# Chunked attention and routed experts on one core: another order in the passage between the two halves, and the last half slot in two banks

## The chip, the cores and the metric

The kernel runs on one core of one Trainium2 chip, in one launch. The metric is the device time of an execution in microseconds; three runs of the kernel before gave a median of 430.8 us (430.32 to 432.37). All five engines (TensorE or PE, VectorE or DVE, ScalarE or ACT, GpSimd or POOL, and SyncE or SP, which here issues DMAs) work in the order in which the code emits their instructions: each engine takes its own instructions strictly one after the other and waits on semaphores for the others.

## The reference

The first half is attention in chunks: 4 batches, 8 heads, 768 rows, head dimension 64. A chunk of 32 queries sees 8 memory keys and at most 56 keys of its neighbourhood. The second half sends each of the 3072 rows (512 wide) to one of 8 experts, the one with the largest logit, and multiplies its output by the softmax weight of that expert.

```
for c in range(nc):                       # 24 chunks of 32
    k_full = concat(mem_k, k_ctx); v_full = concat(mem_v, v_ctx)
    scores = scale * q_c @ k_full.T
    a = exp(scores - max); a = a / (sum(a) + 1e-9)
    out[:, :, chunk] = a @ v_full
...
logits = x @ w_gate + modality_bias[modality_id]
e_idx = argmax(logits); gate_w = softmax(logits)[e_idx]
for e in range(8):
    h = relu(x[e_idx == e] @ w1[e])       # 512 -> 1024
    out[e_idx == e] = gate_w * (h @ w2[e])  # 1024 -> 512
```

## The kernel before

**Attention.** Two heads make a unit, so there are 16 units (`NU`), each in two halves; the loop at line 970 runs over the 32 halves and two steps more. In step i PE computes the scores of half i (`scores`, L328), turns the scores of half i-1 (`trans_p`, L345), turns the finished output of half i-2 (`trans_x`, L382) and multiplies half i-1 with its values (`attend`, L357). DVE subtracts the maximum (`less_max`, L336 and L339) and divides by the sums (`normalize`, L365 to L370, which writes `xb`). ACT takes the exponential (`PT`) and copies banks. POOL copies overlapping values inside a unit's value tile (`share_v`, L271), places the memory keys (`mem_keys`, L302) and stores finished rows to DRAM (`store_x`, L375). Value loads (`load_v`), query and key loads (`load_qk`) and all weights are issued by SP. `warm` (L283) puts products on an idle tile into PE's queue.

**Routing.** After the fourth unit of a batch its route is worked out by a generator (`route`, L529), of which the attention loop takes a few steps at a time (`pump`, L393). A step "full" marks a place where PE has work to emit. For the third batch (`b == B - 2`) the steps are: logits (L534, L543), the ranks of the tokens by a product with a triangle of ones (L575 to L580), on DVE `pick`, `rank`, `eb`, `first` (L583 to L598), on POOL five small operations that turn `first` into the register of the most frequent expert (L600 to L604), then `hi`, `lo`, `ac`, six pairs of indicator rows `l`, `a` (L670, L673: the first `NPOOL` = 2 pairs on POOL, the rest on DVE), the product of these that gives the table of tokens (L683), and its subtraction on DVE (`table`, L687). `gates` (L610) works out the gate values.

**Slots.** The second half works in slots of 256 tokens of one expert. A slot gathers its rows by an indirect DMA on POOL's queue (`gather`, L768: `ix`, `gx`, then two transfers into `xg`), turns them on PE (`trans`, L817), and splits them into a high and a low part (`xt`: ACT L819, DVE L820). Each weight tile is split too (`conv`: ACT L755 writes `wh`, DVE L756 writes `wl`). `mm1_first(f)` (L844) makes 12 products of 256 columns for one of 8 pieces of the hidden layer, its results go through ACT and DVE (L845, L846); `mm2` (L856) makes 48 products of 512 columns; ACT multiplies by the gate (L860) and POOL scatters the rows (L861). Slot 0 takes the most frequent expert of the first three batches, so that it can start before attention has ended: its table is the third batch's. `second` (L696) picks the expert of slot 1, and the rest of the routing runs beside slot 0 (`further`, L1132). Slots 1 to 11 follow (`slot`, L1180); `last_mm2` (L1251) ends slot 11, which is the last work of this input.

**What sets the order around the change.** No scheduler decides: the calls in the loop body and behind it are the order. PSUM tiles named `tr` rotate over four banks (`bank`, L84), `sc` and `av` over two each. For slot 0 the loop calls `gather(0)` at the end of step n-3, and `trans(0)`, `trans(1)` in step n, where they stand in PE's queue behind `trans_x` of half 30. `mm1_first(0)` and `(1)` follow the last `attend`.

Of the kernel before, what the change touches and what calls it, by code (L numbers as in the profile page):

```python
# [45 lines left out]
def tile_chunk_attention_top1_moe(  # L46
# [330 lines left out]
    def trans_x(u, hf):  # L377
        xb = xbs[u]
        t = bank()
        warm(t, {(NU - 2, 0): 3, (NU - 2, 1): 2, (NU - 1, 0): 2}.get((u, hf), 0))  # L380
        for i in range(3):
            nc.tensor.transpose(t[:, i * P:(i + 1) * P], xb[:, 3 * hf + i, :], ident)  # L382
        if hf == 0:
            xTs[u] = xall[:, u % 5]
        nc.scalar.copy(xTs[u][:, 384 * hf:384 * hf + 384], t[:, 0:384])
        if hf == 1 and not NU - 3 <= u < NU - 1:
            store_x(u)
# [141 lines left out]
    def route(b):  # L529
# [58 lines left out]
        if b == B - 2:  # L588

            cb, eb, oha = [sm.tile([P, E], F32, name=name, bufs=1) for name in ("cb", "eb", "oha")]  # L590
            top, ia, ib = [sm.tile([P, 1], F32, name=name, bufs=1) for name in ("top", "ia", "ib")]

            chosen.extend((cb, eb, oha, top, ia, ib))
            nc.scalar.copy(cb, rk[:, NT, :])
            pool, first = nc.gpsimd, sm.tile([P, 1], F32, name="first", bufs=1)
            nc.vector.scalar_tensor_tensor(eb, rk[:, NT, :], float(E), rev[:, 0], op0=ALU.mult, op1=ALU.add)
            yield "v"
            nc.vector.reduce_max(first, eb, axis=AX.X)  # L598
            yield "v"
            pool.tensor_scalar(top, first, 1.0 / E, -0.53125, op0=ALU.mult, op1=ALU.add)  # L600
            pool.tensor_scalar(top, top, MAGIC, -MAGIC, op0=ALU.add, op1=ALU.add)
            pool.tensor_scalar(ia, top, -float(E), first, op0=ALU.mult, op1=ALU.add)
            pool.tensor_scalar(regs0[:, 0:1], ia[0:1], -1.0, float(E), op0=ALU.mult, op1=ALU.add)
            pool.tensor_scalar(regs0[:, 1:2], ia[0:1], -float(HI), float(E * HI), op0=ALU.mult, op1=ALU.add)  # L604
# [43 lines left out]
        for t in range(NT):  # L648
# [28 lines left out]
            hot.append((l1, a1))  # L677
        if b == B - 2:
            yield from gates()
        yield "full"  # L680
# [6 lines left out]
        nc.vector.tensor_sub(table[:, 0:192], table[:, 0:192], tb[:, 0:192])  # L687
        yield "v"
        if b < B - 1:
            ts = sm.tile([P, E], F32, name="ts")  # L690
            nc.vector.reduce_sum(ts, oh.rearrange("p t e -> p e t"), axis=AX.X)
            yield "v"
            nc.vector.tensor_add(tot, tot, ts)
            yield "v"
# [275 lines left out]
    for i in range(n + 2):  # L970
# [9 lines left out]
        if i == n - 3:  # L980
            pump(2, late=True)
        if live:
# [14 lines left out]
        if u + 1 < NU and hf == 0:  # L997
# [5 lines left out]
            if u == 1:  # L1003
                blank_v(2)
            pump(1)
            store_k(u + 1, 1, 0, nc.scalar.copy)
# [7 lines left out]
        elif u + 1 < NU:  # L1014
            if u == 0:
                store_k(1, 0, 0, nc.scalar.copy)
            share_v(u + 1)
            trans_q(u + 1)
            store_q(u + 1, 0)
            store_q(u + 1, 1)  # L1020
            pump(3)
        elif live:
            pump(3)
        first = 2 <= i <= n
        if first:
# [3 lines left out]
        if i == n - 5:  # L1029
            pump(12, ("full",), late=True)  # L1030
        if i == n - 2:
            scores(*units[i + 1])
        if i == n:
            trans(0)
            trans(1)
            conv(1)
        if 1 <= i <= n:
            attend(*units[i - 1])
        if i == n - 3:
            while routing:  # L1040
                pump(99, ("full",), late=True)
        if i > n:
# [6 lines left out]
        if i in (n - 5, n - 4):  # L1049
            pump(2, late=True)  # L1050
        if i == n:
            mm1_first(0)
        if i >= n:
# [14 lines left out]
        if i == n - 5:  # L1068
            regroup_q(NU - 1)
        if i < n:  # L1070
            pump(1, ("tiled",))
# [31 lines left out]
        elif (u, hf) == (NU - 1, 1):  # L1103
            conv(0)
            other = second()
# [34 lines left out]
    keep(0)  # L1140
    mm1_first(2)
    for _ in other:
        pass
    gather(1)
    further()
    conv(4)
    mm1_first(3)
# [13 lines left out]
    for f in range(8):  # L1161
# [5 lines left out]
        if f == 5:  # L1167
            load_w(1, 1)
        if f > 2:
            further(2)  # L1170
            conv(f - 3)
        if f in (5, 6):
            trans(f - 5)
    store(0)
# [76 lines left out]
    def last_mm2(s):  # L1251
        tag, i, puts = ("av", "sc")[s % 2], s % 2, []
        for t in range(2):
            po = ps.tile([P, 512], F32, name=tag, tag=tag, bufs=2)
            for f in range(8):
                a, bb = hh[:, f, t * P:(t + 1) * P], hl[:, f, t * P:(t + 1) * P]
                for n, (x, w) in enumerate(((a, wh), (a, wl), (bb, wh))):
                    nc.tensor.matmul(po, x, w[8 + f], start=(f == 0 and n == 0), stop=(f == 7 and n == 2))
            o = hp.tile([P, DM], F32, name=f"o{t}", bufs=2)
            gate = gate_now[i][:, t:t + 1]  # L1260
            nc.scalar.activation(o, po, AF.Copy, scale=gate)
            puts.append(nc.gpsimd.indirect_dma_start(
# [69 lines left out]
```

## Time and profile before

| | |
|---|---|
| median of three runs | 430.8 us (430.32 to 432.37) |
| the profiled execution's own time | 429.93 us |
| its span, first to last instruction | 428.1 us |
| PE busy | 412.1 us, 96% of the span |
| DVE, ACT, POOL busy | 335.0, 300.2, 234.2 us |
| mean granted clock of TensorE | 0.996 |

The profiled execution took 429.93 us: its span of 428.1 us and 1.83 us around it. A busy time is the sum of an engine's instructions; PE's instructions overlap, and the ends of its products are modelled. Attention ends and slot 0 begins between 111 and 138 us of the span, slot 1 begins at 162, the last product starts at 421.3.

### The profile page before, as it was taken

How to read it: one execution, taken by the hardware profiler on the slowest of the kernel's cores; microseconds unless marked ns; L12 is line 12 of the kernel's file. 1: busy time of each engine (PE TensorE's matmuls, PEld its weight loads, DVE VectorE, ACT ScalarE, POOL GpSimd, SP SyncE). 2: the span in 40 equal slices, each digit the busy share in tenths (PEclk: the TensorE clock that was granted, in tenths of full speed). 3: DMA queues.
4: the chain of work that ended last, by engine and by line, in shares of the span. 5: the costliest groups of instructions: out<-in, count | busy, mean ns of one | idle time of the engine just before them, and what ended most of it. 6: DMA issues, size and time to landing. Idle time of an engine off the chain costs nothing.

```text
span 428.1 us, 11395 instructions
## 1 busy us (share of the span) xinstructions
PE 412.1 (96%) x3867; PEld 342.2 (80%) x3870; DVE 335.0 (78%) x800; ACT 300.2 (70%) x597; POOL 234.2 (55%) x320
## 2 busy tenths in 40 slices
PE   7998999999999999999999999999999999999993
PEld 4776788877867888899898888888888778888882
DVE  6899588588787789858979887868985887978750
ACT  7787778687655557557566867868784778878750
POOL 8967678669584409666753466452706566520101
PEclk9999999999999999999999999999999999999998
DMA  9889999999659500335423667979938323320101
GB/s 218 184 217 246 229 273 201 258 255 212 133 132 312 176 2 2 100 99 76 92 82 52 270 192 167 332 207 334 277 143 253 98 72 84 86 64 2 50 3 55
DMA packets 82543, 66.81 MB, mean 156 GB/s; under 512 B 50659, under 2 KB 71339, under 8 KB 82476
## 3 DMA queue, kind: packets, MB, share of 16 engines
q1 hardware_dynamic: 75276, 46.36, 44.4%
q0 software_dynamic: 6784, 19.50, 14.5%
q8 instruction: 33, 0.54, 0.6%
q14 instruction: 34, 0.28, 0.2%
q10 hardware_dynamic: 416, 0.13, 0.1%
HBM read 84.64 MB, written 12.76 MB: 228 GB/s over the span
## 4 chain that ended last, share of the span: by engine, by line
PE 57%; issue 16%; DVE 10%; DMA 6%; ACT 5%; POOL 4%; POOLq 0%; SPq 0%; ACTq 0%; DVEq 0%
PE av L856 11%; PE tr L844 9%; PE sc L856 8%; PE tr L825 7%; PE av L357 4%; PE tr L828 4%; PE sc L328 3%; ACT kbd L320 3%; PE tr L382 2%; PE tr L345 2%; DMA xpm<-xw 2%; PE tr L292 2%; PE tr L310 1%; DMA out_dram<-o,ix_now 1%; POOL xg L765 1%
## 5 line engine op out<-in xcount | busy, mean ns | idle before, releaser
L756 DVE TENSOR_TENSOR w<-raw,w 128x512 fp32r<-128x512 f32 x96 | 67.4, 746 | 4.1 <-ACT w L755 3.6
L825 PE MATMUL tr<-xt,w 128*128 128x512 f32 x256 | 70.3, 396 | 0.0
L856 PE MATMUL av<-wh,h 128*128 128x512 f32 x192 | 62.5, 398 | 0.0
L271 POOL COPY vw<-vw 24x1472 f32<-24x1472 f32 x32 | 45.0, 1408 | 18.9 <-DMA vw<-in_v_dram 17.5
L755 ACT CAST w<-raw 128x512 fp32r<-128x512 f32 x96 | 53.9, 619 | 0.6 <-DMA raw<-in_moe_w_dram 0.6
L856 PE MATMUL sc<-wh,h 128*128 128x512 f32 x160 | 51.7, 398 | 0.0
L825 PEld LDWEIGHTS tr<-xt,w 128*128 128x128 f32 x256 | 44.3, 189 | 7.5 <-DVE hs L834 0.7
L844 PE MATMUL tr<-xt,w 128*128 128x256 f32 x384 | 48.2, 285 | 1.2 <-DVE xt L820 0.7
L844 PEld LDWEIGHTS tr<-xt,w 128*128 128x128 f32 x384 | 46.8, 191 | 2.7 <-DVE xt L820 0.9
L320 ACT COPY kbd<-tr 64x672 f32<-64x672 f32 x57 | 44.6, 782 | 2.9 <-PE tr L314 1.3
L828 PEld LDWEIGHTS tr<-xt,w 128*128 128x128 f32 x256 | 39.3, 189 | 5.4
L856 PEld LDWEIGHTS av<-wh,h 128*128 128x128 f32 x192 | 36.1, 188 | 8.4 <-issue 0.2
L861 POOL DMA_INDIRECT out_dram<-o,ix_now x22 | 24.5, 1112 | 29.8 <-ACT o L860 24.1
L828 PE MATMUL tr<-xt,w 128*128 128x256 f32 x256 | 40.7, 281 | 0.0
L856 PE MATMUL av<-wl,h 128*128 128x512 f32 x96 | 38.1, 397 | 0.2 <-DVE wl L756 0.2
L834 DVE TENSOR_TENSOR hs<-tr,hs 128x256 f32<-128x256 f32 x64 | 26.8, 419 | 14.4 <-ACT hs L831 14.3
L856 PEld LDWEIGHTS sc<-wh,h 128*128 128x128 f32 x160 | 30.1, 188 | 7.1 <-issue 0.2
L835 ACT ACTIVATE h<-hs 128x256 fp32r<-128x256 f32 x64 | 26.8, 419 | 12.7 <-DVE hs L834 11.6
L837 DVE TENSOR_TENSOR wl<-vw,wh 128x512 fp32r<-128x512 f32 x48 | 34.0, 709 | 2.1
L838 DVE SCALAR_TENSOR_TENSOR h<-hs,h 128x256 fp32r<-128x256 f32 x64 | 27.3, 426 | 7.7 <-ACT h L835 7.7
L765 POOL DMA_INDIRECT xg<-xd,gx x24 | 27.6, 1149 | 10.3 <-issue 5.5
L347 ACT ACTIVATE PT<-tr 128x384 f32<-128x384 f32 x32 | 15.8, 495 | 23.2 <-PE tr L345 23.0
(265 smaller groups left out, 911.1 us busy)
## 6 DMA issues: line engine op xcount, KB each, us to landing
raw<-in_moe_w_dram SPq DMA_DIRECT2D x96, 256.0 KB
vw<-in_moe_w_dram SPq DMA_DIRECT2D x72, 256.0 KB
k<-in_k_dram SPq DMA_DIRECT2D x16, 384.0 KB
q<-in_q_dram SPq DMA_DIRECT2D x16, 384.0 KB
xd<-xb POOLq DMA_DIRECT2D x16, 384.0 KB, 5.9
kbd<-in_moe_w_dram SPq DMA_DIRECT2D x24, 256.0 KB
vw<-in_v_dram SPq DMA_DIRECT2D x32, 184.0 KB
xall<-in_moe_w_dram SPq DMA_DIRECT2D x4, 1024.0 KB
```

The lines of the kernel that those rows point to most:

```text
L271: nc.gpsimd.tensor_copy(vw[r0:r0 + 24, h, 1:NCH, 0:D], vw[r0 + 32:r0 + 56, h, 0:NCH - 1, 0:D])
L320: copy(dst.rearrange("p c (i j) -> p c i j", j=2)[:, :, :, j], win)
L755: nc.scalar.copy(wh[i], raw[i])
L756: (eng or nc.vector).tensor_sub(wl[i], raw[i], wh[i].bitcast(F32))
L765: nc.gpsimd.indirect_dma_start(out=xg[t][:, part], out_offset=None, in_=rows, in_offset=bass.IndirectOffsetOnAxis(ap=gx[:, t:t + 1], axis=0))
L825: nc.tensor.matmul(ph, wh[f][:, c * P:(c + 1) * P], xt[:, c].rearrange("p a n -> p (a n)"), start=(c == 0), stop=False, skip_group_check=True)
L828: nc.tensor.matmul(ph[:, 0:256], wl[f][:, c * P:(c + 1) * P], xth[:, c], start=False, stop=(c == 3), skip_group_check=True)
L834: nc.vector.tensor_add(hs, ph[:, 0:256], hs)
L837: nc.vector.tensor_sub(wl[w], raw[w], wh[w].bitcast(F32))
L838: nc.vector.scalar_tensor_tensor(hl[:, f], hs, 0.0, hh[:, f].bitcast(F32), op0=ALU.max, op1=ALU.subtract)
L844: nc.tensor.matmul(ph, w[f][:, c * P:(c + 1) * P], x[:, c, :], start=(n == 0), stop=(n == 11))
L856: nc.tensor.matmul(pos[t], x, w[8 + f], start=(f == 0 and n == 0), stop=(f == 7 and n == 2))
```

## The change

The change touches the order of work in four places, and one computation.

1. The third batch's route. The ranks (L575 to L580), and the eight DVE steps behind them, are taken at the end of step n-6, one step sooner, ahead of that step's `less_max`; the copy of `cb` on ACT no longer stands ahead of `eb`. The table's product is taken in step n-3 ahead of `trans_q`, and `gates` stands behind the table instead of ahead of it. `share_v` of unit 14 is emitted one step sooner.
2. Slot 0's rows. `trans(0)` and `trans(1)` move from step n to step n-1, ahead of `trans_x` of half 29; `conv(0)` moves to step n-2; `mm1_first(0)` stands ahead of the last `attend`. Four of the seven products of `warm` at the end are taken out.
3. Slot 0's own order: `conv(4)` ahead of the rest of `second`, and at its end `trans` for slot 1 ahead of that step's `further` and `conv`.
4. `last_mm2`: the second half of the tokens is computed as two pieces of 256 columns in two banks, each with its own eviction into one output tile, instead of one piece of 512.

```diff
-        warm(t, {(NU - 2, 0): 3, (NU - 2, 1): 2, (NU - 1, 0): 2}.get((u, hf), 0))
+        warm(t, {(NU - 2, 0): 3}.get((u, hf), 0))
...
-            nc.scalar.copy(cb, rk[:, NT, :])
             pool, first = nc.gpsimd, sm.tile([P, 1], F32, name="first", bufs=1)
...
             nc.vector.reduce_max(first, eb, axis=AX.X)
             yield "v"
+            nc.scalar.copy(cb, rk[:, NT, :])
...
-        if b == B - 2:
-            yield from gates()
         yield "full"
...
         nc.vector.tensor_sub(table[:, 0:192], table[:, 0:192], tb[:, 0:192])
         yield "v"
+        if b == B - 2:
+            yield from gates()
...
         if i == n - 3:
-            pump(2, late=True)
+            pump(99, late=True)
+            pump(1, ("full",), late=True)
...
+            if u == NU - 3:
+                share_v(u + 1)
...
-            share_v(u + 1)
+            if u != NU - 3:
+                share_v(u + 1)
...
-        first = 2 <= i <= n
+        first = 2 <= i < n
+        if i == n - 1:
+            trans(0)
+            trans(1)
...
         if i == n - 5:
-            pump(12, ("full",), late=True)
+            pump(8, late=True)
         if i == n - 2:
             scores(*units[i + 1])
+            conv(0)
         if i == n:
-            trans(0)
-            trans(1)
+            mm1_first(0)
             conv(1)
...
-        if i == n:
-            mm1_first(0)
...
-        if i < n:
+        if i == n - 6:
+            pump(8, ("full",), late=True)
+        elif i < n:
             pump(1, ("tiled",))
...
     mm1_first(2)
+    conv(4)
     for _ in other:
         pass
     gather(1)
     further()
-    conv(4)
     mm1_first(3)
...
+        if f in (5, 6):
+            trans(f - 5)
         if f > 2:
             further(2)
             conv(f - 3)
-        if f in (5, 6):
-            trans(f - 5)
     store(0)
...
+            for part in range(1 + t):
+                cols = slice(DM * part // (1 + t), DM * (part + 1) // (1 + t))
+                tag = ("sc", "av")[part]
+                po = ps.tile([P, 512], F32, name=tag, tag=tag, bufs=2)[:, 0:DM // (1 + t)]
...
+                        nc.tensor.matmul(po, x, w[8 + f][:, cols], start=(f == 0 and n == 0), stop=(f == 7 and n == 2))
+                nc.scalar.activation(o[:, cols], po, AF.Copy, scale=gate_now[i][:, t:t + 1])
```

On POOL, in the third batch's route (`kbd_111` and `vw_114` are key and value tiles of the last units, `xd` the store of finished rows, `first` the route's result on which the five operations from L600 work):

```order
 L302 COPY kbd_110<-memT 64x24x8 x2
-L302 COPY kbd_111<-memT 64x24x8 x2
 L271 COPY vw_114<-vw_114 24x23x64 x2
-L375 DMA xd<-xb 128x6x128
 L600 TENSOR_SCALAR top<-first 128x1
...
 L604 TENSOR_SCALAR regs_161<-ia 1x1
+L302 COPY kbd_111<-memT 64x24x8 x2
+L375 DMA xd<-xb 128x6x128
 L670 TENSOR_SCALAR l_2417<-iota_146,lo 128x130
```

The copies of `vw_114` stand ahead of the memory keys of the last unit and of one store, and these two now stand behind the five operations on `first`; what follows them up to `gather(0)` keeps its order.

On PE, from the gathered rows' transposes to the first logits (before):

```order
L817 MATMUL tr<-ident,xg_2603 128x128
L357 MATMUL av<-vw_112,PT 32x130 x12
L844 MATMUL tr<-xt,w_2605 128x256 x4
L844 MATMUL tr<-xt,w_2606 128x256 x4
L844 MATMUL tr<-xt,w_2605 128x256 x8
L844 MATMUL tr<-xt,w_2606 128x256 x4
L844 MATMUL tr<-xt,w_2605 128x256 x4
L382 MATMUL tr<-ident,xb 128x128 x3
```

The same in the changed kernel:

```order
L817 MATMUL tr<-ident,xg_2603 128x128
L382 MATMUL tr<-ident,xb 128x128 x3
L357 MATMUL av<-vw_112,PT 32x130 x12
L345 MATMUL tr<-ident,sb 128x128 x3
L844 MATMUL tr<-xt,w_2605 128x256 x4
L844 MATMUL tr<-xt,w_2606 128x256 x4
L844 MATMUL tr<-xt,w_2605 128x256 x4
L357 MATMUL av<-vw_112,PT 32x130 x12
L382 MATMUL tr<-ident,xb 128x128 x3
L844 MATMUL tr<-xt,w_2605 128x256 x4
L844 MATMUL tr<-xt,w_2606 128x256 x4
L844 MATMUL tr<-xt,w_2605 128x256 x4
```

Between the gathered rows and `mm1_first(0)` there now stand one `trans_x`, one `attend` and one `trans_p` that stood ahead of them, and a further `trans_x` stands between `mm1_first(0)` and `(1)`.

On DVE, at the end of slot 0, ahead of slot 1's first products (before):

```order
L643 TENSOR_TENSOR ac<-c_3029,hi 128x6
L756 TENSOR_TENSOR w_2606<-raw_2611,w_2605 128x512
L820 TENSOR_TENSOR xt<-tr,xt 128x2x256
L613 TENSOR_REDUCE s_3209<-rex 128x3x2
L615 TENSOR_SCALAR sx<-s_3209 128x6
L756 TENSOR_TENSOR w_2606<-raw_2612,w_2605 128x512
L820 TENSOR_TENSOR xt<-tr,xt 128x2x256
L618 RECIPROCAL gt<-sx 128x24
```

The same in the changed kernel:

```order
L643 TENSOR_TENSOR ac<-c_3025,hi 128x6
L756 TENSOR_TENSOR w_2606<-raw_2611,w_2605 128x512
L820 TENSOR_TENSOR xt<-tr,xt 128x2x256
L613 TENSOR_REDUCE s_3212<-rex 128x3x2
L615 TENSOR_SCALAR sx<-s_3212 128x6
L756 TENSOR_TENSOR w_2606<-raw_2612,w_2605 128x512
L618 RECIPROCAL gt<-sx 128x24
```

The one `xt` left in this stretch is the second of the two (`trans(1)`); the first stands some twenty rows further up. Two small operations and one weight tile's `wl` no longer stand ahead of the second.

## Rows read from the trace of the kernel before

**Rows 1.** Windows: PE, PEld, DVE, ACT, POOL busy, clock, DMA share, GB/s.
```profile
165.00:232.00 67.00, 67.00 (x428) 60.59 (x427) 55.02 (x113) 43.49 (x88) 42.90 (x53) 1.00 0.33 80
232.00:411.00 179.00, 178.63 (x1051) 148.82 (x1050) 145.43 (x289) 137.70 (x295) 79.22 (x99) 1.00 0.54 158
...
424.70:425.70 1.00, 0.00 (x0) 0.00 (x0) 0.00 (x0) 0.00 (x0) 0.00 (x0) 0.64 0.27 102
```

**Rows 2.** Waits of PE, 138 to 165 us: total us, times, longest.
```profile
PE tr L844 <- DVE xt L820: 0.7, 1, 0.7
PE tr L844 <- DVE w L756: 0.5, 1, 0.5
```

**Rows 3.** Chain of waits, 131 to 137 us: start us, us, what.
```profile
127.24 4.26 DMA xg<-xd,gx
...
131.54 0.98 PE tr L817 x7
132.53 0.80 PE av L357 x24
133.33 3.07 PE tr L844 x24
...
136.43 0.38 ACT h L845
```

**Rows 4.** Timeline of PE before slot 0: start us, us, instruction, idle before.
```profile
127.10 0.55 PE L345 MATMUL tr<-ident,sb 128*128 128x128 f32 x3
...
130.76 0.55 PE L382 MATMUL tr<-ident,xb 128*128 128x128 f32 x3 [0.20 <-DVE xb L370]
131.14 1.39 PE L817 MATMUL tr<-ident,xg 128*128 128x128 f32 x8
```

**Rows 5.** Timeline of POOL, 111 to 125 us.
```profile
111.57 0.74 POOL L302 COPY kbd<-memT 64x192 f32<-64x192 f32 x2 [4.52 <-PE sc L328]
112.37 2.88 POOL L271 COPY vw<-vw 24x1472 f32<-24x1472 f32 x2
115.20 0.83 POOL L375 DMA_DIRECT2D xd<-xb  x1
...
124.27 0.18 POOL L775 CAST ix<-table 128x2 int32 x1
```

**Rows 6.** Timeline of DVE, 111 to 116 us.
```profile
111.81 0.55 DVE L336 TENSOR_REDUCE mx<-sc 128x6 f32<-128x384 f32 x1
...
114.12 0.21 DVE L583 TENSOR_TENSOR pick<-tr,oh 128x48 f32<-128x48 f32 x1 [1.17 <-PE tr L580]
...
114.94 0.17 DVE L596 SCALAR_TENSOR_TENSOR eb<-tr,rev 128x8 f32<-128x8 f32 x1 [0.38 <-ACT cb L594]
115.15 0.16 DVE L598 TENSOR_REDUCE first<-eb 128x1 f32<-128x8 f32 x1
```

**Rows 7.** Line 765 at 144.0 to 145.5 us: the gather's time to landing.
```profile
DMA to landing us min/median/max: 3.4/3.4/3.5
```

**Rows 8.** Timeline of DVE before slot 1.
```profile
162.20 0.19 DVE L613 TENSOR_REDUCE s<-rex 128x6 f32<-128x48 f32 x1
...
163.12 0.68 DVE L820 TENSOR_TENSOR xt<-tr,xt 128x512 fp32r<-128x512 f32 x1
```

**Rows 9.** Chain of waits, 187 to 222 us.
```profile
187.13 11.51 PE tr L844 x96
198.65 7.00 PE av L856 x30
```

**Rows 10.** Timeline of all engines at the end.
```profile
421.29 0.40 PE L1258 MATMUL sc<-wh,h 128*128 128x512 f32 x1
421.77 0.69 ACT L1261 ACTIVATE o<-sc,gate_now 128x512 f32<-128x512 f32 x1 [4.91 <-PE sc L1258]
```

**Rows 11.** Timeline of PE at the start.
```profile
1.25 3.59 PE L102 MATMUL tr<-idle 128*128 128x512 bf16 x8 [1.25 <-DVE zero L116]
...
7.71 1.03 PE L965 MATMUL sc<-idle 128*128 128x512 bf16 x4
```

More of the change, by code (lines that the diff above doesn't have):

```diff
@@ L1040, in tile_chunk_attention_top1_moe @@
             while routing:
-                pump(99, ("full",), late=True)
+                pump(99, late=True)
         if i > n:
@@ L1103, in tile_chunk_attention_top1_moe @@
         elif (u, hf) == (NU - 1, 1):
-            conv(0)
             other = second()
@@ L1251, in last_mm2 @@
     def last_mm2(s):
-        tag, i, puts = ("av", "sc")[s % 2], s % 2, []
+        i, puts = s % 2, []
         for t in range(2):
[L1254 to L1258, printed above, removed]
-            o = hp.tile([P, DM], F32, name=f"o{t}", bufs=2)
-            gate = gate_now[i][:, t:t + 1]
-            nc.scalar.activation(o, po, AF.Copy, scale=gate)
+            o = hp.tile([P, DM], F32, name=f"o{t}", bufs=2)
+            for part in range(1 + t):
+                cols = slice(DM * part // (1 + t), DM * (part + 1) // (1 + t))
+                tag = ("sc", "av")[part]
+                po = ps.tile([P, 512], F32, name=tag, tag=tag, bufs=2)[:, 0:DM // (1 + t)]
+                for f in range(8):
+                    a, bb = hh[:, f, t * P:(t + 1) * P], hl[:, f, t * P:(t + 1) * P]
+                    for n, (x, w) in enumerate(((a, wh), (a, wl), (bb, wh))):
+                        nc.tensor.matmul(po, x, w[8 + f][:, cols], start=(f == 0 and n == 0), stop=(f == 7 and n == 2))
+                nc.scalar.activation(o[:, cols], po, AF.Copy, scale=gate_now[i][:, t:t + 1])
             puts.append(nc.gpsimd.indirect_dma_start(
```

## The prediction

> **What bounds the kernel now.** I read the busy times by windows first. From 165 us to the end of the last slot's first half PE is busy in 67.00 of 67 us and then in 178.63 of 179 [rows 1], so nothing behind 165 us can be had by order alone: what the change can gain there is only in the last eviction. The loss lies ahead of it, where attention hands over to slot 0. The waits of PE there are two: 0.7 us for `xt` of slot 1 and 0.5 us for one `w` of slot 0, both for DVE [rows 2]. The chain shows the third: the second transfer of slot 0's gather is issued at 127.24 and lands 4.26 us later, and only then PE turns the rows (0.98 us), does the last `attend` (0.80) and the first two pieces of the hidden layer (3.07) [rows 3]. The timeline shows what PE does meanwhile: it reached the gathered rows at 131.14, after warm-up products and waits for `xb` [rows 4]. So the time at which slot 0 begins is the gather's landing, and the gather hangs on POOL: its instructions follow one another without a gap from 111.57 to `ix` at 124.27 [rows 5]. POOL, not the table on DVE, is what the gather waits for.
>
> **The gather, sooner.** POOL's unbroken run is 12.70 us (111.57 to 124.27) [rows 5]. The pair of value copies that is moved out of it takes 115.20 - 112.37 = 2.83 us and goes into the 4.52 us in which POOL waits ahead of 111.57 for the scores [rows 5]. What is left, 9.87 us, can now begin only when `first` is there. DVE is free at 111.81, where it starts `mx` today [rows 6]; in its place come `pick` to `first`, which today take from 114.12 to 115.31, of which 0.38 is a wait for the copy of `cb` that no longer stands ahead [rows 6]: 111.81 + 0.81 = 112.62, with 0.08 us to wake POOL 112.70. So `ix` is at 122.57, 1.70 us sooner. From `ix` to the second transfer's landing I keep today's 7.27 us (124.27 to 127.24, and 4.26), since the same weight loads are issued right behind it: 129.84 instead of 131.54. DVE's eight steps and the indicator rows delay `less_max` of that step by some 1.5 us; its result is needed at the next `trans_p`, a step later, so this is hidden by PE's other work. The table is then ready before POOL comes to it; were it late, the gather would be late by as much.
>
> **What now stands behind the gather.** PE takes its queue in order, and the transposes moved a step up. Behind them, and ahead of the first logits, there now stand two `trans_x` (0.38 us each, from 130.76 to 131.14 [rows 4]), one `attend` (0.80 [rows 3]) and one `trans_p` (three transposes again, 0.38): 1.94 us that today fill the time until the landing. So the end of `mm1_first(2)`, the first place where both orders have done the same work, moves by -1.70 + 1.94 = +0.24 us. That is the point of this forecast: the gather comes sooner by less than the work that is put behind it. The warm-up products that go cost nothing and give nothing, since PE stands in a wait there either way: `trans_p` of half 30, now the last work ahead of the gathered rows, began at 127.10 [rows 4], so PE would be ready for them at about 126.8 to 127.6 and wait 2.2 to 3.0 us. `conv(0)` on ACT and DVE, the moved `cb` copy, the ranks' and the table's place in PE's queue and the gates behind the table all end inside this wait; without it each would cost its own length, 0.2 to 0.7 us. `mm1_first(0)` ahead of the last `attend` changes the order of equal work; it could make PE wait about 0.1 us for `conv(1)`, which now follows the first piece's activation on ACT.
> The bounds. The landing took 3.4 us for slot 1's gather [rows 7]; with that the place moves by -0.62 instead of +0.24. If POOL's chain gave nothing, it moves by +1.94. If the rows were there as soon as PE is ready, about 127.2, PE alone would set the place: 127.2 - 131.54 + 1.94 = -2.4. I take +0.1, near the end that today's own gather gives, as POOL's part is read instruction by instruction.
>
> **Slot 0's order.** `conv(4)` ahead of the rest of `second` puts the `wl` that PE waits 0.5 us for ahead of eight small DVE operations, about 1 us; the wait goes, -0.5 [rows 2]. What is late next is slot 1's register by 0.6 us, and slot 1's rows are used more than 10 us later. `trans` ahead of `further` and `conv` takes two small operations and one `wl` from ahead of the second `xt`: it starts 163.12 - 162.20 = 0.92 us sooner [rows 8], the wait was 0.7 [rows 2], so it goes with 0.2 us to spare: -0.7. The `wl` put behind it is the fourth piece's, used some 4 us later. Both stay between these and zero; below that nothing speaks, as PE has no other wait there.
>
> **The last half slot.** 24 products of 512 columns take 0.233 us each (7.00 for 30), products of 256 with a weight load each 0.120 (11.51 for 96) [rows 9]: 48 x 0.120 - 24 x 0.233 = +0.16. The eviction behind the last product, 0.69 us for 512 columns [rows 10], becomes one of 256, for which the nearest ACT row is 0.38 [rows 3]: -0.31. Together -0.15; the first piece's eviction lies beside the second's products. If the pieces paid as much as a 512-column product, it would be +5.3, but the hidden layer's 96 rows are the same form.
>
> **Sum.** +0.1 - 0.5 - 0.7 - 0.15 = -1.25 us, call it -1.3. The profiled execution took 429.93, so it would take 428.6; the median of the runs is 430.8, 0.9 above it, and I predict against that: **429.5 us**. Its own range, with a landing of 3.4 us on one side and one of the two DVE waits kept on the other, is 428.4 to 430.5. A measurement of this kernel tells about 0.5% (2.15 us) from no change.
>
> **Rivals.**
> Early rows. The gather lands well before 129.8 because POOL's operations run faster beside other DVE work and the transfer meets less traffic. For it: the 3.4 us [rows 7]. Against it: POOL's chain is the same instructions. With 3.4 us and 0.6 us less on POOL (an estimate, half of what is missing to PE's own limit) it lands at 128.4, the place moves by -1.2, the sum is -2.6: 428.2; at PE's limit -3.8: 427.0.
> The clock falls, ending slower. For 2.2 to 3.0 us PE would do nothing but one or two transposes, with four of the seven warm-up products gone. At the end of the run PE has done nothing since about 421.7, and in the window from 424.70 the granted clock is 0.64 [rows 1, 10]: if it was 1.00 and then 0.50, it fell after 0.28 us of that window, 3.3 us after the last product. So the wait must grow by only 0.3 us or more to reach that. The price: at the start eight idle products took 3.59 us where four take 1.03 later [rows 11], 0.43 against 0.21 us each less the last one's tail; 3.4 us of work at the lower level, 1.2 GHz, costs 1.7 us. With a gather 0.5 us later than I think, -1.3 + 0.5 + 1.7 = +0.9: 431.7; twice the stretch at the lower level, +2.6: 433.4. Against it: both longer windows of rows 1 show the full clock, and four products of `warm` are short beside the wait that they fill.
> The Trainium skill, "TensorE: Matmul & The Clock Gate", section "Why this matters for your kernels", also says to avoid pauses between bursts of products, as the clock goes back after one; the end of this trace agrees, and by that rule this change would end as this rival does.
> The gather is no sooner. `share_v` of unit 14 now stands 5 us earlier, and if its value loads have not landed by 109.9 (112.70 - 2.83), all behind it shifts; at today's time for `ix` the place moves by +1.94 and the sum is +0.6: 431.4. Against it: today's pair starts at 112.37 with no wait ahead of it [rows 5], 2.5 us after the time from which it would decide.
>
> **How the numbers follow.** Forecast 0.56, early rows 0.24, clock 0.11, gather no sooner 0.09. Faster by over 0.5% takes -2.15 or more: most of early rows (0.19) and a tenth of the forecast (0.06), 0.25. Slower by over 0.5% takes +2.15: half of the clock's case and what I have overlooked, 0.09. The rest, 0.66, is within. The range 427.4 to 431.6 holds the forecast, the nearer half of early rows and the cases that end slightly slower.
>
> **What would show it.** In the profile after: POOL's `top` at about 112.7 and `ix` at about 122.6; the gather's second landing near 129.8; PE idle for 2 to 3 us ahead of L817; the first logits (L534) within 0.7 us of 138.1; no wait of L844 for `w` and for `xt`; the last ACT eviction near 0.4 us; clock 1.00 through 130 us. Wrong would be a landing before 128.5 or behind 131, a granted clock below 1, or L844 waiting again between 138 and 165.

## The result and the profile after

The changed kernel takes 433.81 us (median of 22 runs) where the kernel before, run beside it on the same chip, takes 431.42 (22 runs): ratio 1.0055, 95% interval 1.0035 to 1.0074, 2.4 us slower. The forecast was 429.5 in a range to 431.6, so it was wrong, and on the wrong side. The profiled execution took 432.98 us, 431.2 of them span, at a mean granted clock of 0.988; before it was 0.996. Ratios and means of the clock below leave out executions more than 1.5% above the fastest of their kernel (three of these 22, two of 13 with parts 1, 3 and 4, at most one of before's in a comparison); medians are over all.

The clock comes first. The windows of the kernel after (busy us of PE, PEld, DVE, ACT and POOL, granted clock, DMA share, GB/s):

```profile
107.00:113.00 6.00, 5.41 (x83) 4.20 (x81) 5.38 (x19) 3.16 (x6) 2.82 (x2) 1.00 0.41 106
113.00:114.00 1.00, 0.34 (x2) 0.34 (x3) 0.86 (x5) 0.98 (x2) 0.66 (x3) 0.91 0.78 177
114.00:117.00 3.00, 3.00 (x37) 2.44 (x39) 1.88 (x6) 1.98 (x6) 2.63 (x8) 0.50 0.36 64
117.00:118.00 1.00, 1.00 (x29) 0.79 (x22) 0.67 (x3) 0.00 (x0) 1.00 (x2) 0.89 0.99 295
...
130.00:131.00 1.00, 0.00 (x0) 0.01 (x1) 0.30 (x1) 0.00 (x0) 1.00 (x6) 0.94 0.97 314
131.00:134.00 3.00, 2.82 (x15) 2.22 (x19) 0.69 (x1) 1.17 (x2) 1.87 (x8) 0.50 1.19 306
134.00:135.00 1.00, 1.00 (x26) 0.78 (x26) 0.69 (x1) 0.48 (x2) 0.00 (x0) 0.85 1.09 356
...
232.00:411.00 179.00, 178.68 (x1048) 148.90 (x1047) 145.69 (x295) 136.52 (x292) 80.30 (x99) 1.00 0.54 159
```

The granted clock is at 0.50, the level of 1.2 GHz, from 114 to 117 and again from 131 to 134 us, with part of the slices beside them. The work lost is at most the length of each slice by what its clock lacks: 0.09 + 1.50 + 0.11 = 1.70 us, and 0.06 + 1.50 + 0.15 = 1.71. It is less where PE had nothing to do, as from 130 to 131 us. From 232 us on PE is as full as before [rows 1]; nothing is lost there. Each fall follows a wait of PE. The waits of PE in the kernel after, 105 to 170 us (us in total, times, longest), and its timeline around the two waits (start us, us, engine, line, operation; in brackets the idle time before and what ended it):

```profile
PE tr L817 <- issue: 2.5, 1, 2.5
PE tr L292 <- ACT kbd L320: 1.0, 1, 1.0
PE tr L844 <- DVE xt L820: 0.7, 1, 0.7
```

```profile
113.66 1.44 PE L292 MATMUL tr<-ident,qr 128*128 128x128 f32 x6 [1.00 <-ACT kbd L320]
...
127.98 0.55 PE L345 MATMUL tr<-ident,sb 128*128 128x128 f32 x3
131.02 0.45 PE L817 MATMUL tr<-ident,xg 128*128 128x128 f32 x1 [2.49 <-issue]
131.62 1.76 PE L817 MATMUL tr<-ident,xg 128*128 128x128 f32 x7 [0.16 <-DMA xg<-xd,gx]
```

The eight turns of the rows (L817) begin at 131.02, where they began at 131.14 before [rows 4]: PE has done its other work sooner and stands 2.65 us. Of the two waits of L844 [rows 2] the one for `w` is gone, the one for `xt` is still there. The chain of the kernel after has the transfer (start us, us, what):

```profile
125.91 5.67 DMA xg<-xd,gx
131.58 0.04 issue
131.62 1.76 PE tr L817 x7
```

It is issued 1.33 us sooner than in [rows 3], takes 5.67 instead of 4.26 us, and lands when it did (131.58 against 131.50). The logits (L534) begin at 141.49 by the timeline, where the forecast had within 0.7 us of 138.1. POOL and DVE of the kernel after show what became of the gather's other end, its issue:

```profile
107.28 2.88 POOL L271 COPY vw<-vw 24x1472 f32<-24x1472 f32 x2 [0.44 <-DMA vw<-in_v_dram]
113.15 0.18 POOL L600 TENSOR_SCALAR top<-first 128x1 f32<-128x1 f32 x1 [2.99 <-DVE h L632]
...
122.94 0.18 POOL L775 CAST ix<-table 128x2 int32 x1 [0.40 <-ACT xall L385]
```

```profile
108.90 1.31 DVE L553 TENSOR_TENSOR l<-l,rmx 128x48 f32<-128x48 f32 x1
110.25 0.21 DVE L557 SCALAR_TENSOR_TENSOR eq<-l,rev 128x48 f32<-128x48 f32 x1
```

The value copies are where the change put them, and beside them one small DVE operation of 128x48, L553, takes 1.31 us; the next of the same size, behind the copies' end at 110.16, takes 0.21. ACT's exponent waits for it, the key copies wait for ACT, and PE's L292 for these. `top` starts at 113.15 instead of the forecast 112.70, `ix` at 122.94 instead of 122.57. POOL waits 0.40 us ahead of `ix`; by the chain it is for the table, whose products (L681) stand on PE behind the slow stretch from 114 us. So the issue came sooner, by 1.3 of the 1.7 us forecast; the landing did not.

The end of the kernel after answers to [rows 10]:

```profile
424.19 0.27 PE L1268 MATMUL av<-wh,h 128*128 128x256 f32 x1
424.51 0.47 ACT L1269 ACTIVATE o<-av,gate_now 128x256 f32<-128x256 f32 x1 [2.31 <-PE av L1268]
425.25 0.98 POOL L1270 DMA_INDIRECT out_dram<-o,ix_now  x1 [4.43 <-ACT o L1269]
```

From the end of PE to the scatter it is 425.25 - 424.46 = 0.79 us.

### The profile page after: what moved, and what is told of

The parts are those of the page before. It is cut to its first block, busy times and chain, and to the rows that moved or that the text cites. A ratio compares the mean times of both kernels' runs of the same rounds, so it can differ in the third digit from the quotient of the medians.

```text
span 431.2 us, 11436 instructions
## 1 busy us (share of the span) xinstructions
PE 413.3 (96%) x3890; PEld 345.5 (80%) x3890; DVE 335.4 (78%) x800; ACT 300.2 (70%) x598; POOL 237.7 (55%) x320
## 4 chain that ended last, share of the span: by engine, by line
PE 60%; issue 15%; DMA 9%; DVE 7%; ACT 4%; POOL 4%; POOLq 1%; ACTq 0%; SPq 0%
PE av L856 12%; PE tr L844 9%; PE sc L856 8%; PE tr L825 7%; PE av L357 5%; PE tr L828 4%; PE sc L328 3%; ACT kbd L320 2%; DMA vw<-in_v_dram 2%; PE tr L382 2%; DMA xg<-xd,gx 2%; PE tr L345 2%; PE tr L292 2%; DMA xpm<-xw 2%; DMA out_dram<-o,ix_now 2%
## 5 line engine op out<-in xcount | busy, mean ns | idle before, releaser
L271 POOL COPY vw<-vw 24x1472 f32<-24x1472 f32 x32 | 45.8, 1430 | 18.3 <-DMA vw<-in_v_dram 17.1
L844 PE MATMUL tr<-xt,w 128*128 128x256 f32 x384 | 48.5, 285 | 0.7 <-DVE xt L820 0.7
L844 PEld LDWEIGHTS tr<-xt,w 128*128 128x128 f32 x384 | 46.9, 191 | 2.1 <-DVE xt L820 0.9
```

Source lines behind the costliest of these rows:

```text
L271: nc.gpsimd.tensor_copy(vw[r0:r0 + 24, h, 1:NCH, 0:D], vw[r0 + 32:r0 + 56, h, 0:NCH - 1, 0:D])
L844: nc.tensor.matmul(ph, w[f][:, c * P:(c + 1) * P], x[:, c, :], start=(n == 0), stop=(n == 11))
```

## The experiments

The theory after this reading: part 2 makes PE wait for the gather with its own work queued behind, and the clock falls behind the wait; parts 3 and 4 gain what was worked out, less the `xt`. The rivals: part 1's value copies, which stretch DVE; and the gates' store, which moved behind the table and now stands 1.5 us ahead of the transfer that got slower. Each kernel was run beside the kernel before on the same chip. "Lost to the clock" is the mean over the runs of the span times one minus its mean granted clock; before has 1.4 us in all three comparisons. That 1.4 is no loss of work: in the profile of before the clock is 1.00 up to 424.70 us, then falls [rows 1], and stays at 0.50 to the end of the span, where PE has no product left:

```profile
425.70:426.70 1.00, 0.00 (x0) 0.00 (x0) 0.00 (x0) 0.00 (x0) 0.00 (x0) 0.50 0.06 16
```

So what counts is the part above 1.4, and that too is an upper bound, as it holds stretches in which PE waits anyway.

| kernel | median us | ratio to before [95%] | lost to the clock, us |
|---|---|---|---|
| changed kernel (parts 1 to 4) | 433.81 | 1.0055 [1.0035, 1.0074] | 3.5 |
| parts 3, 4 | 430.51 | 0.9984 [0.9951, 1.0017] | 2.0 |
| parts 1, 3, 4 | 429.58 | 0.9980 [0.9956, 1.0004] | 1.8 |
| parts 2, 3, 4 | 432.68 | 1.0055 [1.0031, 1.0079] | 2.7 |
| parts 2, 3, 4, 14 idle products | 431.50 | 1.0030 [1.0011, 1.0048] | 1.9 |
| parts 2, 3, 4, turns later | 430.59 | 1.0014 [0.9990, 1.0037] | 1.6 |
| changed, 12 idle products | 432.11 | 1.0036 [1.0013, 1.0060] | 1.9 |
| changed, gates ahead of the table | 435.20 | 1.0106 [1.0064, 1.0147] | 4.3 |
| parts 1, 3, 4, value copies back | 432.49 | 1.0043 [1.0018, 1.0067] | 2.9 |
| before, four idle products out | 430.50 | 1.0005 [0.9974, 1.0035] | 1.5 |
| parts 3, 4, turns behind `further` | 429.78, 429.48 | 0.9967 [0.9944, 0.9989], 0.9981 [0.9955, 1.0007] | 1.3, 1.9 |
| parts 1, 3, 4, turns behind `further` | 429.57 | 0.9989 [0.9963, 1.0014] | 2.2 |

**Parts 3 and 4 alone.** The two hunks of slot 0 and `last_mm2`, on the kernel before.

> The kernel before, with parts 3 and 4 of the change alone (slot 0's order and the last half's two banks). Theory: parts 1 and 2 cost the time, so this kernel keeps the logits of slot 0 (L534) at 138.1 us, L844's wait of 0.5 us for w goes (-0.5), the end is 0.2 to 0.25 shorter, and the wait for slot 1's xt stays, because the first of the two turns now waits in DVE's queue for PE's transposes (about 0.7 us of waiting on DVE, then 0.5 to 0.7 on PE). Sum -0.7 us, ratio 0.998. Rival, that slot 0's order or the two banks are among what slows: +0.3 us or more, and L844 waits longer than 0.7 us for xt, or the last products' pitch is above 0.120. Granted clock 1.00 from 100 to 140 us by the theory.

0.9984, as the theory had it, though the interval holds no difference too. PE does not wait for `w`; it waits 0.7 us for `xt`, as before. DVE in this kernel shows why:

```profile
159.93 0.69 DVE L820 TENSOR_TENSOR xt<-tr,xt 128x512 fp32r<-128x512 f32 x1 [0.85 <-ACT xt L819]
163.04 0.68 DVE L756 TENSOR_TENSOR w<-raw,w 128x512 fp32r<-128x512 f32 x1
163.64 0.68 DVE L820 TENSOR_TENSOR xt<-tr,xt 128x512 fp32r<-128x512 f32 x1
```

The first `xt` comes to the head of DVE's queue before PE has turned its rows; DVE stands 0.85 us, and all behind it, the small operations of `further` and the second `xt` too, is as late as before, counted from the turns of slot 1.

**Slot 1's turns between.**

```
         if f > 2:
             further(2)
+        if f in (5, 6):
+            trans(f - 5)
+        if f > 2:
             conv(f - 3)
-        if f in (5, 6):
-            trans(f - 5)
```

> Parts 3 and 4 on the kernel before, but with slot 1's turns between `further` and `conv`, not ahead of both. Theory that the gain of 0.7 us was eaten because DVE reached the turn before PE had its transposes done: behind the small operations of `further` DVE waits less than 0.2 us there, xt is ready 0.4 to 0.7 us sooner than with the turns ahead of both, and L844's wait for it falls under 0.3: about -1.2 us against before, ratio 0.997. Rival, that the wait for xt is set by when PE makes the transposes and not by DVE's order: L844 still waits 0.6 to 0.7 us for xt, and the time equals that of parts 3 and 4 as they stand.

0.9967, and the wait is gone, as the theory had it. PE in this kernel has no idle time ahead of slot 1's products, and DVE's two `xt` stand 1.5 us apart without a wait:

```profile
158.92 0.69 DVE L820 TENSOR_TENSOR xt<-tr,xt 128x512 fp32r<-128x512 f32 x1
159.52 0.68 DVE L756 TENSOR_TENSOR w<-raw,w 128x512 fp32r<-128x512 f32 x1
160.12 0.20 DVE L613 TENSOR_REDUCE s<-rex 128x6 f32<-128x48 f32 x1
160.43 0.68 DVE L820 TENSOR_TENSOR xt<-tr,xt 128x512 fp32r<-128x512 f32 x1
```

It was measured a second time:

> Once more the kernel before with parts 3 and 4, slot 1's turns between `further` and `conv`. If the 0.9967 of the other look holds, the ratio is 0.995 to 0.998 again, and this is the version that beats both kernels. If that was luck of the loads in the first 110 us, it comes out at 0.999 or above, since order in slot 0 and the last eviction can give 1.25 us (0.997) at most.

0.9981, on the edge of what was expected. Weighted by their intervals the two ratios give 0.9973 [0.9956, 0.9990], 1.2 us less than before: of all versions measured only this one has an interval wholly below before.

**Gates ahead of the table again**, in the changed kernel.

```
+        if b == B - 2:
+            yield from gates()
         yield "full"
...
-        if b == B - 2:
-            yield from gates()
```

> The changed kernel with the gates ahead of the table again (as before). Theory: the gather's second transfer took 5.7 us instead of 4.3 because the store of gates that stood 1 us ahead of the first transfer was still in flight beside it; with the store a microsecond or more sooner the second lands about 4.3 us after its issue. If ix keeps its 122.9, that is 130.2, PE's wait ahead of L817 falls from 2.65 to about 1.3 us, the clock does not fall behind it, and mm1_first(2) ends 2.5 to 3 us sooner than in the changed kernel (138.5 to 139): -2.5 us against it, about level with before. Rival, that the raw weight loads behind the gather or the reads of rows themselves set the landing: it stays near 131.6 whatever stands ahead, the time within 0.5 us of the changed kernel. A second rival: the gates ahead of the table delay the table on DVE by their own length, ix comes 0.5 to 1 us later, and half of the gain goes.

It fell: 1.0106, slower than the changed kernel. The second transfer landed 4.1 us after its issue, but `ix` came at 125.78 and PE waited 2.75 + 0.39 us. The clock stayed, with the seven turns at 0.98 us:

```profile
132.21 0.30 PE L817 MATMUL tr<-ident,xg 128*128 128x128 f32 x1 [2.75 <-issue]
132.89 0.98 PE L817 MATMUL tr<-ident,xg 128*128 128x128 f32 x7 [0.39 <-DMA xg<-xd,gx]
```

In this profile the value copies waited for their loads and met other DVE operations (POOL, then DVE):

```profile
111.08 2.88 POOL L271 COPY vw<-vw 24x1472 f32<-24x1472 f32 x2 [2.81 <-DMA vw<-in_v_dram]
```

```profile
111.12 1.42 DVE L557 SCALAR_TENSOR_TENSOR eq<-l,rev 128x48 f32<-128x48 f32 x1
112.58 0.20 DVE L560 TENSOR_REDUCE me<-eq 128x6 f32<-128x48 f32 x1
112.82 1.20 DVE L563 TENSOR_TENSOR oh<-rev,me 128x48 bf16<-128x48 f32 x1
```

Both stretched operations have two inputs; the reduction between them, with one, takes its 0.20 us. The landing itself came out as the theory had it, 4.09 us for the forecast 4.3, and the time still did not follow: `ix` stood 16.9 us behind the third batch's L543 (125.78 - 108.92), where the changed kernel has 16.0 (122.94 - 106.94), as the second rival had it. Whether the store made the slow landing stays open. The chains have 4.26 us for the second transfer in before, 4.92 with parts 3 and 4 alone and 3.62 with parts 2 to 4, all three with the store 3.7 us ahead of it, so 1.3 us of spread needs no store; but the longest, 5.67, is also the one with the store closest, 1.46 us ahead (124.45). What sets it was not settled.

**Idle products in PE's wait**, 12 ahead of the first turn in the changed kernel; and 14 of them with parts 2, 3 and 4.

```
-    def trans(half):
-        t = bank().rearrange("p (c n) -> p c n", c=2)
+    def trans(half, fill=0):
+        t = bank()
+        warm(t, fill)
+        t = t.rearrange("p (c n) -> p c n", c=2)
...
-            trans(0)
+            trans(0, 12)
```

> The changed kernel with 12 idle products of 512 columns (0.21 to 0.23 us each, 2.6 us) between trans_p of half 30 and the first turn of gathered rows, where PE waits. Theory, that the wait of 2.65 us costs mostly by the clock that falls behind it: granted clock 1.00 from 128 to 136, L817's eight transposes and the work to L534 at 2.4 GHz, mm1_first(2) ends about 1.4 us sooner than in the changed kernel (140.1 instead of 141.5), -1.4 us in all. Rival, that the clock costs nothing here since PE waits again for other engines: 141.3 or later, no difference. The first fall of the clock, at 114 to 117 us, stays in both.

> Parts 2, 3 and 4 without part 1 (1.0055 before), with 14 idle products of 512 columns ahead of the turns of slot 0's rows, 3.1 us of PE's wait of 3.5 to 4. Theory, that part 2 costs twice, 1.7 us by the work that it puts behind the rows and 1.3 us by the clock that falls behind the wait: with the wait filled the mean loss to the clock goes from 2.7 to 1.5 us (before's own), the ratio to 1.002 to 1.003, and no more, as the work is still behind. Rival, that the order costs nothing by itself and all is the clock: ratio 0.999. Second rival, that the idle products delay the rows: loss 1.5, ratio 1.0055 still.

In the first the loss to the clock goes from 3.5 to 1.9 us and the ratio from 1.0055 to 1.0036: 0.8 us of time for 1.6 us of clock, where 1.4 us was expected. PE's timeline of it (one record of the twelve is missing):

```profile
126.93 2.75 PE L283 MATMUL tr<-idle 128*128 128x512 bf16 x11
129.52 0.30 PE L819 MATMUL tr<-ident,xg 128*128 128x128 f32 x1
130.87 0.98 PE L819 MATMUL tr<-ident,xg 128*128 128x128 f32 x7 [1.05 <-DMA xg<-xd,gx]
```

Seven turns take 0.98 us, not 1.76: the clock stayed. The second goes from 1.0055 to 1.0030, 1.1 us, with the loss from 2.7 to 1.9 (1.5 was expected). Each of the two gains has an interval of some 1.3 us on either side, both together are 0.9 us with 0.9 on either side: filling the wait returns about a microsecond, and most of the slowdown stays. The first expected 114 to 117 us to stay low; in its profile the clock was 1.00 there, with a wait of 0.4 us at L292.

**Part 2 without part 1, and part 1 without part 2.** Part 2 on the kernel before, in its core (the places of `conv(0)` and `mm1_first(0)` and the four idle products change with it, as in the whole diff; the other is the changed kernel with all of this undone):

```
-        first = 2 <= i <= n
+        first = 2 <= i < n
+        if i == n - 1:
+            trans(0)
+            trans(1)
...
         if i == n:
-            trans(0)
-            trans(1)
+            mm1_first(0)
             conv(1)
```

> Parts 2, 3 and 4 without part 1: the turns of slot 0's rows stand a step earlier on PE, while ranks, value copies, table and gather keep their old places. Theory, that part 2 makes PE wait for the gather with its own work queued behind, and that the clock falls behind that wait: PE waits about 3.5 us ahead of L817, since the rows land about 24.4 us after the third batch's L543 as before; the 1.94 us of work behind them are added, and in most runs the granted clock falls for 3 to 4 us (loss over all runs, as span times one minus the mean clock, near 3 us where before has 1.45). With -0.75 from parts 3 and 4: +1.2 by the order and +1.5 by the clock, +2.7 us against before, ratio 1.006. Rival, that part 1's collisions on DVE and POOL are what slows and part 2 is harmless: within 0.5 us of parts 3 and 4 alone, 0.998 to 1.000, and the loss to the clock at 1.5.

> Parts 1, 3 and 4 without part 2: ranks, value copies, table and gather sooner, but PE turns slot 0's rows where it did before, behind its other work and all seven warm products. Theory: no wait of PE for the gather is left, since PE comes to the rows about 24 us behind L543 and they land by then; the loss to the clock is near before's 1.45 us plus what the wait at the turns of q for unit 14 (L292, 0.4 to 1.0 us) brings now and then, 2 us; the work up to L534 takes 30.6 us from L543, up to 1 us less than in before. Time 430 to 431, ratio 0.997 to 1.000. Rival, that part 1 slows by itself because POOL's value copies stand beside DVE's operations with two inputs: PE's wait at L292 or L577 is 1 us or more, L534 is 31.5 us or more behind L543, ratio 1.003.

These two, with the neither (0.9984) and the both (1.0055), settle it: part 2 adds 0.007 with or without part 1, and part 1 adds nothing with or without part 2 that these intervals can tell (1.3 us on either side with part 2, 1.8 without). Without part 2 a sooner gather has little to give: in before PE comes to the gathered rows at 131.14 and needs 1.39 us for the eight turns [rows 4], where they take 1.04 if all rows are there, so PE lost only 0.35 us to the gather (0.78 in the profile of parts 3 and 4 alone). The eight turns without a wait, with parts 3 and 4 and slot 1's turns between:

```profile
130.21 1.04 PE L817 MATMUL tr<-ident,xg 128*128 128x128 f32 x8
```

In the profile of parts 2, 3 and 4 the first turn waits 1.85 us and the rest 1.07:

```profile
128.50 0.33 PE L817 MATMUL tr<-ident,xg 128*128 128x128 f32 x1 [1.85 <-DMA xg<-xd,gx]
129.90 1.37 PE L817 MATMUL tr<-ident,xg 128*128 128x128 f32 x7 [1.07 <-DMA xg<-xd,gx]
```

and the granted clock goes to 0.56 right behind (its windows):

```profile
129.00:130.00 1.00, 0.10 (x1) 0.10 (x2) 0.00 (x0) 0.00 (x0) 1.00 (x7) 1.00 0.97 293
130.00:133.00 3.00, 3.00 (x34) 2.49 (x34) 1.38 (x2) 1.65 (x3) 1.86 (x7) 0.56 1.00 259
```

**The turns later.** With parts 2, 3 and 4, `trans(0)` and `trans(1)` moved behind `trans_x` and `attend` of the same step.

```
-        if i == n - 1:
-            trans(0)
-            trans(1)
...
         if 1 <= i <= n:
             attend(*units[i - 1])
+        if i == n - 1:
+            trans(0)
+            trans(1)
```

> Parts 2, 3 and 4 without part 1, but the turns of slot 0's rows stand behind `trans_x` and `attend` of that step, no longer ahead of them: 0.38 + 0.80 = 1.18 us of work less behind the gather, and PE waits 1.18 us less for it. Theory: -1.2 us by order against the version with the turns ahead, and most of the 1.3 us of the clock too, as the wait is then about 1.7 to 2.3 us: ratio 0.999 to 1.002. Rival, that the slowdown is elsewhere in part 2 (`mm1_first` ahead of the last `attend`, `conv(0)` sooner): ratio stays at 1.005.

1.0014, as expected: PE waits 0.80 us for the second transfer only, and the loss to the clock is 1.6. So what stands behind the rows is the larger part of part 2's cost. The 0.003 that is left against parts 3 and 4 alone has an interval of 0.004 on either side; one `trans_p` and one `trans_x`, 0.76 us, still stand behind the rows, and `mm1_first(0)` and `conv(0)` were not tried by themselves.

**Value copies back in their old place**, with parts 1, 3 and 4.

```
-            if u == NU - 3:
-                share_v(u + 1)
...
-            if u != NU - 3:
-                share_v(u + 1)
+            share_v(u + 1)
```

> As parts 1, 3 and 4 without part 2, but the value copies of unit 14 stay in their old place, behind POOL's `top` chain. Theory, that it is the copies beside DVE's two-input operations that stretch those: L553, L557 and L563 take 0.21 us each again, L577 does not wait, and L292 waits as in before (0.55); `ix` comes about 1 us later than in before, as the copies stand in POOL's run again. PE then waits 0.5 to 1 us for the rows; time within 1 us of parts 1, 3 and 4. Rival, that the stretching comes from DVE's own order or from the transfers: an operation among L553, L557 and L563 takes 1.2 us or more here too.

On what stretches DVE the theory held: with no copy beside them the same operations take 0.2 us.

```profile
112.04 0.21 DVE L553 TENSOR_TENSOR l<-l,rmx 128x48 f32<-128x48 f32 x1
112.29 0.21 DVE L557 SCALAR_TENSOR_TENSOR eq<-l,rev 128x48 f32<-128x48 f32 x1
...
112.77 0.21 DVE L563 TENSOR_TENSOR oh<-rev,me 128x48 bf16<-128x48 f32 x1
```

On the time it missed: 1.0043, by the ratios some 2.7 us above parts 1, 3 and 4, and PE did not wait for the rows. Part 1 put the table's products (L681) ahead of other work in PE's queue; POOL now makes their inputs later, and PE waits 0.49 and 1.22 us for them, with the clock at 0.58 behind it:

```profile
123.40 0.35 PE L681 MATMUL tr<-a,l 128*128 128x192 f32 x1 [0.49 <-POOL a L673]
124.98 0.94 PE L681 MATMUL tr<-a,l 128*128 128x192 f32 x5 [1.22 <-POOL a L673]
```

```profile
125.00:128.00 3.00, 3.00 (x20) 2.65 (x24) 1.94 (x7) 1.13 (x3) 2.87 (x3) 0.58 0.87 227
```

**Four idle products out of before**, the first hunk of the diff alone.

```
-        warm(t, {(NU - 2, 0): 3, (NU - 2, 1): 2, (NU - 1, 0): 2}.get((u, hf), 0))
+        warm(t, {(NU - 2, 0): 3}.get((u, hf), 0))
```

> The kernel before without four of its seven idle products ahead of the last `trans_x` (two and two), the four that the change takes out. The prediction said that they cost nothing and give nothing. By it the time is that of before within 0.3 us and the mean clock the same (loss 1.45 us). Rival, that they hold the clock: PE then has pauses of 0.6 to 0.8 us there, three in a row within 4 us, the granted clock falls between 128 and 136 in a good part of the runs, the loss grows by 0.5 to 1.5 us, ratio 1.001 to 1.004.

1.0005 and 1.5 us lost: within 1.3 us on either side they give nothing there, as the prediction had it. In the changed kernel, where PE's wait is longer, no run puts these four back; the twelve in the wait did give something.

**Parts 1, 3 and 4 with the turns behind `further`,** by the edit shown above under "Slot 1's turns between".

> Parts 1, 3 and 4 without part 2, slot 1's turns between `further` and `conv`. Theory, that part 1 gives nothing at the median, as PE without part 2 comes to the rows when they are there anyway, and makes the time spread more, as the value copies of unit 14 now wait for loads that landed between 107.3 and 113 us: ratio 0.996 to 0.998 with single runs 5 us or more above the fastest, mean loss to the clock above 2 us. Rival, that the sooner gather is worth its 1 us once the other parts are right: ratio 0.994 or below.

0.9989, above the 0.996 to 0.998 expected, and the slowest execution stands 4.6 us above the fastest, where 5 or more was expected: the sooner gather is worth nothing that the time shows, here either. In its profile the logits begin 29.7 us behind the third batch's L543 (136.91 - 107.18), where parts 3 and 4 with the same turns have 30.6 (136.79 - 106.21); but over the runs the loss to the clock is 2.2 us, not 1.3 to 1.9. POOL in this profile waits for the value loads:

```profile
110.25 3.10 POOL L271 COPY vw<-vw 24x1472 f32<-24x1472 f32 x2 [3.01 <-DMA vw<-in_v_dram]
113.45 0.18 POOL L600 TENSOR_SCALAR top<-first 128x1 f32<-128x1 f32 x1
```

## Why the prediction was wrong, step by step

**"The gather, sooner", -1.70: the step that failed first.** The rows landed at 131.58 instead of 131.50, so +0.08. The issue did come sooner, by 1.33 us; the other term of that step, the landing kept at today's 4.26, was 5.67. Over the runs the whole step is worth nothing: with part 2 in both, the ratio is 1.0055 with part 1 and without it, within 1.3 us. The landing was 3.6 to 5.7 us over the profiles. One transfer seen once is no constant; the range should have had this spread on both sides, not only the 3.4 of slot 1's gather. Why it was slow in the changed kernel stays open. The reading behind the step, that slot 0 begins at the gather's landing, held in before by 0.35 us only; it was part 2 that made the whole landing count.

The step also put the value copies into a wait of POOL without asking whether their loads are there; that today's pair "starts at 112.37 with no wait" only says that they land before 112.37 [rows 5]. In the profiles of the changed kernel, with gates first, with idle products, and of parts 1, 3 and 4 with the turns behind `further` the copies began at 107.28, 111.08, 110.50 and 110.25, each after a wait for the load; the rival "the gather is no sooner" had named 109.9. What that cost was less than its price: with idle products and with the turns behind `further`, `ix` still stood 16.0 us behind L543, as in the changed kernel, against 17.1 in before. That rival was right that the step gives nothing, and not for its reason.

**"What now stands behind the gather", +1.94: right.** With the clock held by idle products part 2 costs 1.0030 - 0.9984 without part 1, 2.0 us, and 1.0036 - 0.9980 with it, 2.4 us; each pair of intervals leaves some 1.5 us of doubt. So 1.94 is held, not measured closely. The prediction had the order's cost right and set against it a gain that did not come.

**The clock: the rival "the clock falls" came true, and its condition was the error.** The prediction took from the end of the run how long after the last product the clock fell there [rows 1, 10], and held its own wait of 2.2 to 3.0 us to be short of that by 0.3. Here the clock fell behind waits of 2.65 and of 1.00 us. That one stretch at the end, where no product follows, could not say how short a wait may be. The Trainium skill, "TensorE: Matmul & The Clock Gate", section "Why this matters for your kernels", warns of pauses between bursts of products; the runs agree that the clock can fall behind one, and differ in that these waits are shorter than the pauses it names, as the forecast wait was too. The rival's price, 1.7 us a stretch, is what both stretches show as an upper bound (1.70 and 1.71), but the first lies ahead of PE's wait of 2.65 us and by the chain could cost no more than the 0.40 us by which `ix` waited. Over the runs the loss grew by 2.1 us, and filling the wait gave back 0.8 and 1.1. That this rival's 433.4 for two stretches lies so near 433.8 is luck: it had the waits for `w` and `xt` both gone and a gather 0.5 us late.

**DVE's and POOL's work "hidden by PE's other work": wrong.** It was costed at nothing with the durations of before, and those of the small two-input operations hold only while POOL does not copy. L553 took 1.31 us for 0.21, and PE waited 1.00 us at L292 (0.55 before). The trace of before had the warning, a still smaller two-input sum beside copies of the same kind, which takes 0.17 us at 72.58, with no copy beside it:

```profile
102.61 2.88 POOL L271 COPY vw<-vw 24x1472 f32<-24x1472 f32 x2
102.92 1.12 DVE L693 TENSOR_TENSOR tot<-tot,ts 128x8 bf16<-128x8 bf16 x1
```

The Trainium skill, "SBUF — State Buffer", section "Who interferes with whom", says that a DVE instruction with two inputs in SBUF contends with a GpSimd instruction that reads SBUF; the rows agree, with the two-input operations at 1.31, 1.42 and 1.20 us and the one-input reduction between them at 0.20.

**Slot 0's order.** `conv(4)`: right, the wait for `w` is gone. The `xt`: -0.7 did not come. I took two small operations away from ahead of the second `xt` and asked how much sooner it could start, but not whether the first had its rows: DVE stood 0.84 us in the changed kernel (0.85 with parts 3 and 4 alone). With the turns one place later it came.

**The last half slot: right**, with 0.79 us from PE's end to the scatter. In before the scatter follows the rows of [rows 10] at

```profile
422.73 0.98 POOL L1262 DMA_INDIRECT out_dram<-o,ix_now  x1 [4.62 <-ACT o L1261]
```

which is 422.73 - 421.69 = 1.04 us behind PE's end. So the eviction gave -0.25, where -0.31 was forecast for it, and -0.15 with the products' own +0.16.

In the two profiles the account closes up to the first logits, which begin 3.41 us later (141.49 against 138.08): +0.08 for the landing, the forecast's +1.94 for the work behind it, and +1.34 for the clock behind 131.62 (2.38 us at 0.50, and 0.15) make 3.36. The forecast had +0.1 there. So of the 3.7 us between -1.3 and +2.4 the gather is some 1.8, the clock 1.3 in this profile and about 0.9 by the idle products, and the `xt` 0.7. The gather's share is shown by the landing and by part 1's worth of nothing; how much of the rest is the clock is known to about a microsecond.

The prediction's own signs of being wrong all showed: a landing behind 131, a clock below 1, and L844 waiting for `xt`.

## What to carry to other kernels

Work that a queue in order holds ahead of a late arrival is worth its length, and more if the clock falls behind the wait: move an arrival's consumer up only when the arrival has been seen to come sooner in several executions. A wait of an engine seen in a trace is a place for other work only if that work's own inputs are there: look for the time at which its loads land, not for the time at which it ran. And price a VectorE operation by the row that had the same neighbour on GpSimd; here before's own trace had one, at 1.12 us.

## What the runs showed of the hardware

- The clock went to its lower level behind a wait of PE of 1.00 us (at 113.66) and of 2.65 us (at 131.62) in the changed kernel, and of 1.85 and 1.07 us with parts 2, 3 and 4; not behind 2.75 and 0.39 us in the profile with gates first, where PE's seven turns took 0.98 us. The length of one wait does not decide it; what does was not settled.
- Beside two GpSimd copies of 24x1472 (1.41 us each) a 128x48 VectorE operation with two inputs took 1.20 to 1.42 us for 0.21, until a copy ended, and one of 128x8 took 1.12 us for 0.17.
- The second transfer of slot 0's indirect gather took 3.6 to 5.7 us from issue to landing, with the same code and rows, in eight kernels that differ around it.
